# Two attention blocks side by side: VectorE's part of phi placed behind the next scores, the first q and k written in pieces, 25600 columns ahead of tile 0, and A's last q chains moved

## The chip, the cores and the metric

The kernel runs on one core of a Trainium2 chip. Its engines run side by side, each with its own queue of instructions, and wait for each other through semaphores: TensorE (PE in the profile, its weight loads PEld), VectorE (DVE), ScalarE (ACT), GpSimd (POOL) and SyncE (SP, which here issues most DMAs). The metric is the time of one execution on the device in microseconds, the median of the timed runs. The profiler's span runs from the first to the last instruction and is a little shorter than that time.

## The reference

Two independent attention blocks A and B work on inputs of 2048 tokens by 640 columns, with 32 heads of 20 channels. Their outputs stand side by side in a result of 2048 by 1280.

```python
# A: causal attention in a window of 256
qkv = (x @ wqkv).reshape(B, S, 3, H, Dh)
scores = einsum("bhqd,bhkd->bhqk", q, k) * (Dh ** -0.5)
mask = (i - j >= 0) & (i - j < 256)
o = softmax(where(mask, scores, -1e9)) @ v
out_A = o.reshape(B, S, D) @ wo

# B: linear attention over all tokens
phi = lambda t: where(t > 0, t + 1, exp(t)) + 1e-6
pq, pk = phi(q), phi(k)
kv = einsum("bhsd,bhse->bhde", pk, v);  z = einsum("bhsd->bhd", pk)
o = einsum("bhqd,bhde->bhqe", pq, kv) / (einsum("bhqd,bhd->bhq", pq, z)[..., None] + 1e-6)
out_B = o.reshape(B, S, D) @ wo
```

## The kernel before

**Stages of 512 tokens.** Both blocks are cut into NS = 4 stages of SB = 512 tokens (TPS = 4 blocks of 128). A product with a weight matrix is a *chain* (`chain`, L201): KT = 5 matmuls that add up in one bank of PSUM, up to 512 columns wide. The pool `dps` has three such banks. `bank()` hands out the next one, so the chain of bank n+3 cannot start before bank n has been read. `evac` copies a bank to SBUF, on VectorE (L192) or, near the end, in turn with ScalarE (L190).

**A's tiles.** `a_rows` makes q or k of a stage with channels on the partitions: five chains of 128 channels, evacuated into the tile `st`. `bounce` writes `st` to a scratch in DRAM (L267), and four DMAs read it back (L271) into `qpad` or `kpad`, where each head has its own rows. `a_v` makes v. The scores of a stage are cut into units, 90 in all (`tiles_of`): eight or sixteen small matmuls into the only tile `S_ps` (L574), one Exp of ScalarE over 128x2048 into `p` (L582), a mask by GpSimd (`affine_select`, L596), and two units later 16 matmuls `O_ps` of p with v (L618). Where a group of units ends, VectorE takes the reciprocal of the sums (L640) and multiplies (`otokA`, L641). After the last group of a stage `otokA` is transposed by DMA into `oT` (L652), and `a_out` multiplies with wo.

**B's work.** `b_kv(s)` makes k in token rows with phi, v, and adds the products of both to `kv_acc`. `b_q(s)` makes q with phi, channels on the partitions, and a DMA transpose `tok<-phi` (L498) of each of its five chains. `b_den`, `quotients` (L534 and the DMA transposes of L537), `b_merge` and `b_out` divide and project. `kv_ready` runs steps of GpSimd and DMA between the chains of b_q(0).

**phi.** `phi` issues the Exp of a bank on ScalarE (L210) at once. Its remaining part, two instructions of VectorE (L214, `e<-e`; L217, `phi<-dense,e`), is put into the list `later`. `flush` issues what is in that list. Before, `evac` called it behind its copy, and `phi` behind its own Exp; so the pair of a bank came right after the next evacuation or the next phi. The pair reads the bank, so the bank comes free only after it.

**The order of the work** is written out by hand. `fill` is one long generator over all chains. First come a_v(0) and q and k of A's stage 0. Then `take(EARLY)` runs EARLY columns of `fill` ahead of the first scores. From there on, each unit takes an equal share of what is left: `rate = (FILL - TAIL - ...) / 90` columns behind the O_ps matmuls of the unit two before it. `spread` mixes quarters of the transposing loads of the next x (L689) into a generator, one each `step` yields; `even` interleaves two generators bank by bank; `drip` does so with the reads of `bounce`. SP's queue is in order, so a DMA that waits holds all behind it.

**The start.** SP loads x of A's stage 0 in two halves and A's weights by thirds. TensorE first runs 40 dummy matmuls on the identity (`warm_up`, L150), which GpSimd makes; then it transposes x (L134) and starts a_v(0).

**The end.** `b_out(3)` and `a_out_last` (four output DMAs of SP, L673) run behind the last units.

Of the kernel before, what the change touches and what calls it, by code (L numbers as in the profile page):

```python
# [9 lines left out]
P = 128  # L10
# [6 lines left out]
H = 32  # L17
# [6 lines left out]
EARLY = 33280  # L24
FILL = 350080
# [29 lines left out]
def kernel(  # L55
# [52 lines left out]
    def load_w(n, src, i, eng):  # L108
        wv = src.rearrange("(kt p) n -> p kt n", p=P)
        eng.dma_start(  # L110
            out=w_sb[n][:, :, i * D : (i + 1) * D], in_=wv[:, :, i * D : (i + 1) * D]
        )
# [33 lines left out]
    def warm_up():  # L146

        ps = dps.tile([P, SB], F32, name="dense")
        for _ in range(40):
            nc.tensor.matmul(ps[:, 0:P], lhsT=ident[:], rhs=ident[:], start=True, stop=True)  # L150
# [24 lines left out]
    later = []  # L175

    def flush():

        while later:
            later.pop(0)()  # L180
# [3 lines left out]
    def evac(dst, src, to=None):  # L184
# [8 lines left out]
        flush()  # L193

    def bank():
        return dps.tile([P, SB], F32, name="dense")
# [10 lines left out]
    def phi(dst, src, view=lambda t: t[:], then=None):  # L207

        e = ep.tile([P, SB], BF16, name="e")
        nc.scalar.activation(out=view(e), in_=src, func=ACT.Exp)  # L210
        flush()
# [11 lines left out]
        later.append(rest)  # L223
# [38 lines left out]
    def bounce(n, s, st, dst):  # L262


        scratch = tc.dram_tile([D, SB], BF16, name=f"{n}_scr{s}")
        eng = nc.scalar if s == 0 else nc.sync
        eng.dma_start(out=scratch.rearrange("(c p) n -> p c n", p=P), in_=st[:])  # L267
# [21 lines left out]
    def a_rows(n, s):  # L289
        base = 0 if n == "q" else D  # L290
        st = stp.tile([P, KT, SB], BF16, name="st")
        for c in range(KT):
# [7 lines left out]
            evac(st[:, c, :], ps[:])  # L300
            if c == KT - 1:
                pad, pl, name = (q_pad, qp, "qpad") if n == "q" else (k_pad, kp, "kpad")
                pad[s] = pl.tile([P, NG, SB], BF16, name=name)
                bounce(n, s, st, pad[s])
# [15 lines left out]
    def v_proj(n, xt, dst):  # L320
        hh = H // 2
        for tb in range(TPS):
            for i in range(2):
                ps = bank()
                yield from chain(
                    ps[:, 0 : hh * DH],
                    lambda kt: xt[:, kt, tb * P : (tb + 1) * P],
                    lambda kt: w_sb[n][:, kt, 2 * D + i * hh * DH : 2 * D + (i + 1) * hh * DH],
                    hh * DH,
                )  # L330
                evac(
                    dst[:, tb, i * hh : (i + 1) * hh, 0:DH],
                    ps[:, 0 : hh * DH].rearrange("p (h d) -> p h d", d=DH),
                )
                yield End(hh * DH)
# [380 lines left out]
    for i in range(2):  # L716
        load_w("A", A_wqkv, i, nc.sync)
# [120 lines left out]
```

## Time and profile before

| | |
|---|---|
| median of three timed runs | 281.84 us (279.88, 281.84, 284.75) |
| the profiled execution | 280.25 us |
| its span | 278.5 us |
| PE busy | 266.9 us, 96% |
| ACT, DVE, POOL busy | 201.8, 172.7, 163.1 us |
| the Exp of a unit (L582) | 90 x 1875 ns |
| O_ps matmuls (L618) | 1440, 50.9 us |
| phi on VectorE (L214, L217) | 40 x 0.39 us and 40 x 0.69 us |
| first scores at | 38.12 us |

A line of the profile names the source line of the kernel, the engine, the operation and `written<-read` tiles; `x8` is a count, `[0.79 <-DMA xB]` an idle time ahead of the instruction and what ended it. A `q` behind an engine's name (SPq, ACTq) marks its sequencer, which issues DMAs. A window has, for each engine, its busy time and count. The timed runs of this kernel spread over 1.7%.

### The profile page before, as it was taken

The numbers are of one execution on the slowest core, as the hardware profiler recorded it, in microseconds if no ns is written. First come the engines' busy times: TensorE is split into PE (matmuls) and PEld (weight loads), VectorE is DVE, ScalarE is ACT, GpSimd is POOL, SyncE is SP. The second block draws the span as 40 slices with busy tenths as digits, with TensorE's granted clock in tenths as the row PEclk, the third lists the DMA queues.
The fourth block names the chain that finished last, engine by engine and source line by source line (L and its number), as shares of the span: only waits on it lengthen the run. The fifth ranks groups of instructions, "written<-read, shape, count | busy, mean of one in ns | idle before, by whom it ended". The sixth has DMA issues, their size and how long they took to land.

```text
span 278.5 us, 8218 instructions
## 1 busy us (share of the span) xinstructions
PE 266.9 (96%) x3474; PEld 155.3 (56%) x3516; DVE 172.7 (62%) x336; ACT 201.8 (72%) x231; POOL 163.1 (59%) x204
## 2 busy tenths in 40 slices
PE   7999999999999999999999899999999999999995
PEld 7744465665665654565664354465644564456542
DVE  0656665657757555554566576987688767866821
ACT  1200039989989887889989899778889889998432
POOL 5000017667656667776669956676687778777710
PEclk9999999999999999999999999999999999999999
DMA  7997596949532994541016624599979744940886
GB/s 248 305 308 215 157 233 164 175 89 201 158 74 47 138 126 113 142 120 34 2 26 120 106 50 101 133 163 192 173 121 151 111 134 126 116 117 28 167 193 209
DMA packets 81214, 38.88 MB, mean 140 GB/s; under 512 B 63897, under 2 KB 80281, under 8 KB 81177
## 3 DMA queue, kind: packets, MB, share of 16 engines
q1 hardware_dynamic: 78857, 32.45, 57.7%
q0 software_dynamic: 1008, 4.59, 5.0%
q10 hardware_dynamic: 1312, 1.31, 1.4%
q8 instruction: 27, 0.44, 0.7%
q14 instruction: 10, 0.08, 0.2%
HBM read 12.45 MB, written 10.49 MB: 82 GB/s over the span
## 4 chain that ended last, share of the span: by engine, by line
PE 82%; ACT 7%; DVE 3%; issue 3%; DMA 2%; POOL 1%; DVEq 0%; POOLq 0%; SPq 0%; ACTq 0%
PE dense L201 52%; PE O_ps L618 14%; PE S_ps L574 10%; ACT p L582 6%; PE dense L415 2%; PE dense L150 2%; DMA xA<-vB 1%; DMA xB<-in_B_x_dram 1%; POOL p L596 1%; PE dense L464 1%; DVE otokA L641 1%; ACT e L210 1%; PE dense L134 1%; DVE tok L534 1%; DVE st L192 0%
## 5 line engine op out<-in xcount | busy, mean ns | idle before, releaser
L596 POOL TENSOR_SCALAR_AFFINE_SELECT p<-p 128x512 bf16<-128x512 bf16 (+1 forms) x180 | 150.9, 839 | 100.7 <-ACT p L582 93.6
L582 ACT ACTIVATE p<-S_ps 128x2048 bf16<-128x2048 f32 x90 | 168.7, 1875 | 39.5 <-PE S_ps L574 39.0
L618 PEld LDWEIGHTS <-p 128*128 128x128 bf16 x1440 | 42.3, 96 | 20.2 <-issue 16.9
L618 PE MATMUL O_ps<-vA,p 128*128 128x21 bf16 x1440 | 50.9, 173 | 1.1 <-DVE otokA L641 0.6
L201 PE MATMUL dense<-wB,xB 128*128 128x320 bf16 (+2 forms) x310 | 48.1, 296 | 1.0 <-DVE vB L192 0.3
L201 PE MATMUL dense<-xA,wA 128*128 128x512 bf16 x191 | 45.3, 379 | 0.6
L192 DVE CAST st<-dense 128x512 bf16<-128x512 f32 x40 | 27.5, 690 | 22.5 <-PE dense L201 19.5
L574 PE MATMUL S_ps<-qpad,kpad 20*128 20x256 bf16 (+2 forms) x736 | 35.9, 269 | 0.9 <-ACT p L582 0.4
L192 DVE CAST osb<-dense 128x512 bf16<-128x512 f32 (+1 forms) x35 | 22.5, 642 | 20.7 <-PE dense L201 19.2
L201 PEld LDWEIGHTS <-xA 128*128 128x128 bf16 x320 | 26.5, 97 | 15.1 <-DMA xA<-vB 1.6
L201 PEld LDWEIGHTS <-xB 128*128 128x128 bf16 x320 | 26.0, 97 | 13.3 <-issue 1.3
L574 PEld LDWEIGHTS <-kpad 20*128 20x128 bf16 x736 | 12.7, 92 | 30.5 <-issue 29.0
L201 PEld LDWEIGHTS <-wA 128*128 128x128 bf16 x200 | 18.5, 97 | 19.9
L217 DVE SCALAR_TENSOR_TENSOR phi<-dense,e 128x512 bf16<-128x512 f32 x40 | 27.7, 692 | 1.4
L567 ACT ACTIVATE p<-ident 1x1 bf16<-1x1 bf16 x90 | 16.9, 188 | 15.4 <-DVE st L192 15.4
L201 PE MATMUL dense<-wB,xA 128*128 128x512 bf16 (+1 forms) x155 | 24.5, 296 | 1.0 <-DMA xA<-vB 0.6
L201 PE MATMUL dense<-xB,wB 128*128 128x512 bf16 x89 | 24.2, 378 | 1.3 <-DMA xB<-in_B_x_dram 0.8
L210 ACT ACTIVATE e<-dense 128x512 bf16<-128x512 f32 x40 | 23.6, 593 | 1.3 <-PE dense L201 0.9
L192 DVE CAST vB<-dense 128x320 bf16<-128x320 f32 x32 | 15.3, 489 | 14.7 <-PE dense L201 14.2
L201 PE MATMUL dense<-woA,oT 128*128 128x128 bf16 (+1 forms) x153 | 23.4, 295 | 0.8 <-DVE osb L192 0.5
L201 PE MATMUL dense<-wA,xA 128*128 128x320 bf16 x160 | 23.9, 299 | 0.1
L192 DVE CAST vA<-dense 128x320 bf16<-128x320 f32 x32 | 15.8, 492 | 9.4 <-PE dense L201 9.3
(41 smaller groups left out, 150.4 us busy)
## 6 DMA issues: line engine op xcount, KB each, us to landing
out_dram<-osb POOLq DMA_DIRECT2D x7, 640.0 KB, 4.3
qpad<-q_scr SPq DMA_DIRECT2D x16, 160.0 KB
kpad<-k_scr SPq DMA_DIRECT2D x16, 160.0 KB
wA<-in_A_wqkv_dram SPq DMA_DIRECT2D x3, 800.0 KB
wB<-in_B_wqkv_dram SPq DMA_DIRECT2D x3, 800.0 KB
q_scr<-st SPq DMA_DIRECT2D x3, 640.0 KB
k_scr<-st SPq DMA_DIRECT2D x3, 640.0 KB
woA<-in_A_wo_dram SPq DMA_DIRECT2D x1, 800.0 KB
```

The costliest lines, as they stand in the source:

```text
L134: nc.tensor.transpose(ps[:, c * P : (c + 1) * P], tok[:, tb, c * P : (c + 1) * P], ident[:])
L150: nc.tensor.matmul(ps[:, 0:P], lhsT=ident[:], rhs=ident[:], start=True, stop=True)
L192: nc.vector.tensor_copy(out=dst, in_=src)
L201: nc.tensor.matmul(dst, lhsT=lhs(kt), rhs=rhs(kt), start=(kt == 0), stop=(kt == KT - 1))
L210: nc.scalar.activation(out=view(e), in_=src, func=ACT.Exp)
L217: nc.vector.scalar_tensor_tensor(out=dst, in0=src, scalar=0.0, in1=view(e), op0=ALU.max, op1=ALU.add)
L415: nc.tensor.matmul(pv[:, i, :, :], lhsT=pk[:, tb, c * P : (c + 1) * P], rhs=vB[:, tb, GH * c : GH * c + NHC, :], start=(tb == 0), stop=(tb ...
L567: nc.scalar.activation(out=p_all[0:1, 4 * SB : 4 * SB + 1], in_=ident[0:1, 0:1], func=ACT.Copy)
L574: nc.tensor.matmul(S_ps[:, j, blk * P : blk * P + n], lhsT=kt[32 * j : 32 * j + DH, g, ko : ko + P], rhs=q_pad[s][32 * j : 32 * j + DH, g, ...
L582: nc.scalar.activation(out=p, in_=S_ps[:], func=ACT.Exp, scale=scale)
L596: nc.gpsimd.affine_select(out=v, in_=v, pattern=[[0, 4], [0, b1 - b0], [sgn, P]], compare_op=ALU.is_ge, fill=0.0, base=0 if kind == "D" el ...
L618: nc.tensor.matmul(O_ps[:, slot, j, :], lhsT=p[:, j, b * P : (b + 1) * P], rhs=v_tok[kb // TPS][:, kb % TPS, 4 * gg + j, :], start=(first ...
```

## The change

There are five parts.

1. **phi.** `evac` and `phi` no longer call `flush`. The tile loop calls it right behind each `scores`, ahead of `values`. Each entry of `later` carries the number of its bank, and `bank()` flushes the entries that are two banks old, so that a bank has been read when its turn comes again.
2. **First q and k.** In stage 0, each chunk of 128 channels is written to the scratch by its own DMA of ScalarE's queue, right behind its evacuation, five for q and five for k instead of one each. The reads wait for all five. Other stages are as before.
3. **The start.** The dummies read a zeroed tile (a memset of VectorE, in a buffer of `osb`) instead of the identity; 28 run ahead of the first transposes and 3 behind them. A's v weights come in two halves, the first ahead of the second half of x, and a_v(0) takes the first columns of token blocks 0 and 1 before the others.
4. **Columns.** EARLY falls from 33280 to 25600 columns, and FILL rises by the same 7680: the share of a unit goes from 3668 to 3753 columns.
5. **A's stage 3.** Its five q chains (`banks(early, KT)`) run ahead of b_kv(3), no longer between the chains of b_q(0). The five k chains alternate one by one with b_q(0), and the quarters of B's next x are issued at each of the first yields (step 1, before 4).

The last output of A uses a buffer of `otokA`, no longer of `osb`.

```diff
-EARLY = 33280
-FILL = 350080
+EARLY = 25600
+FILL = 357760
...
-    def warm_up():
-
+    def warm_up(wait):
+
+        z = op.tile([P, TPS, D], BF16, name="osb")
+        nc.vector.memset(z[:, 0, 0:P], 0.0)
         ps = dps.tile([P, SB], F32, name="dense")
-        for _ in range(40):
-            nc.tensor.matmul(ps[:, 0:P], lhsT=ident[:], rhs=ident[:], start=True, stop=True)
+        for n in wait:
+            for _ in range(n):
+                nc.tensor.matmul(
+                    ps[:, 0:P], lhsT=z[:, 0, 0:P], rhs=z[:, 0, 0:P], start=True, stop=True
+                )
+            yield
...
     later = []
-
-    def flush():
-
-        while later:
-            later.pop(0)()
+    begun = [0]
+
+    def flush(before=None):
+
+        while later and (before is None or later[0][0] <= before):
+            later.pop(0)[1]()
...
             nc.vector.tensor_copy(out=dst, in_=src)
-        flush()

     def bank():
+        flush(begun[0] - 2)
+        begun[0] += 1
         return dps.tile([P, SB], F32, name="dense")
...
         nc.scalar.activation(out=view(e), in_=src, func=ACT.Exp)
-        flush()
...
-        later.append(rest)
+        later.append((begun[0], rest))
...
-    def bounce(n, s, st, dst):
-
-
-        scratch = tc.dram_tile([D, SB], BF16, name=f"{n}_scr{s}")
-        eng = nc.scalar if s == 0 else nc.sync
-        eng.dma_start(out=scratch.rearrange("(c p) n -> p c n", p=P), in_=st[:])
+    def bounce(n, s, scratch, st, dst):
+
+
+        if s > 0:
+            nc.sync.dma_start(out=scratch.rearrange("(c p) n -> p c n", p=P), in_=st[:])
...
             evac(st[:, c, :], ps[:])
+            if s == 0:
+                nc.scalar.dma_start(out=scratch[c * P : (c + 1) * P, :], in_=st[:, c, :])
...
+        order = by_tokens
+        if s == 0:
+            order = [(0, 0), (1, 0), (0, 1), (1, 1), (2, 0), (2, 1), (3, 0), (3, 1)]
+        yield from v_proj("A", xA[s], v_tok[s], order)
...
     load_half(0)
-    load_w("A", A_wqkv, 2, nc.sync)
+    load_w("A", A_wqkv, 2, nc.sync, 0, hh * DH)
     load_half(1)
+    load_w("A", A_wqkv, 2, nc.sync, hh * DH, D)
...
-    warm_up()
+    dummies = warm_up((28, 3))
+    next(dummies)
     transposes(0)
+    next(dummies)
...
         k_reads(2, a_v(2)),
+        banks(early, KT),
         b_kv(3),
-        spread(even(q[0], KT, early, 3), [("B", NS + 1)], 4),
+        spread(even(q[0], KT, early, KT), [("B", NS + 1)], 1),
...
         p = scores(okey[0], parts)
+        flush()
```

45 lines of the change are left out of this document (22 added, 23 removed).

## The prediction

> **What bounds the kernel now.** First the busy table, the slices and the chain of the page.
>
> ```profile
> PE 266.9 (96%) x3474; PEld 155.3 (56%) x3516; DVE 172.7 (62%) x336; ACT 201.8 (72%) x231; POOL 163.1 (59%) x204
> ...
> PE   7999999999999999999999899999999999999995
> ...
> PEclk9999999999999999999999999999999999999999
> ...
> PE 82%; ACT 7%; DVE 3%; issue 3%; DMA 2%; POOL 1%; DVEq 0%; POOLq 0%; SPq 0%; ACTq 0%
> ```
>
> TensorE is full in every slice but the first and the last two, and 82% of the chain is its own work. So an edit gains only where TensorE stands still or does work that is no part of the result. The waits of PE name the standing:
>
> ```profile
> PE dense L150 <- POOL ident masks.py:199: 1.4, 1, 1.4
> PE dense L201 <- DMA xB<-in_B_x_dram: 0.8, 1, 0.8
> PE O_ps L618 <- DVE otokA L641: 0.6, 1, 0.6
> PE dense L201 <- DMA xA<-vB: 0.6, 1, 0.6
> PE dense L201 <- DVE osb L192: 0.5, 1, 0.5
> PE O_ps L618 <- POOL p L596: 0.4, 1, 0.4
> ```
>
> They are few and short. Measured from start to start of the matmul records, against the usual 0.216 us of a 512-column matmul, the places that lose over 0.25 us are 93.6 us (0.47), 153.9 (0.57), 157.4 (0.95), 177.1 (0.71), 220.4 (0.65), 255.0 (0.26) and 266.4 (0.72): 4.3 us together. With the head this is all that can be won.
>
> **The head.** Windows over the first microseconds (busy time and count of PE, PEld, DVE, ACT, POOL):
>
> ```profile
> 1.43:5.67 4.24, 4.24 (x41) 4.24 (x42) 0.00 (x0) 0.66 (x1) 2.78 (x5) 1.00 0.88 292
> 5.67:6.99 1.32, 1.27 (x12) 1.00 (x11) 0.49 (x1) 0.01 (x1) 0.00 (x0) 1.00 1.06 377
> 6.99:13.18 6.19, 6.19 (x50) 4.52 (x51) 3.83 (x8) 1.39 (x2) 0.00 (x0) 1.00 1.15 328
> ```
>
> The 40 dummy matmuls take 4.24 us, 0.106 each. After 6.99 us the same 128 columns take 0.056: TensorE runs at half speed until there, and although the column of the granted clock says 1.00, the record of that clock begins only at 6.99. By the packets in the trace the first half of x has landed at 3.47, long before the first transpose at 5.67.
>
> Changed: the dummies no longer wait for the identity (ready at 1.37) but for a memset of VectorE. The other engines' first instructions start at 0.81; the memset is bounded by POOL's first fills (0.10) and VectorE's memset of 220 words (0.24), and the hand-over takes 0.05, so 1.05 is taken. 28 x 0.106 brings the first transpose to 4.02 (was 5.67), still behind the landing by 0.55. Ten transposes (1.06) and three dummies (0.32) end at 5.40; xA's first copy, 0.78 + 0.49 behind the first transpose as before, is ready at 5.34. The first chain starts at 5.40, not 6.99: 1.59 earlier, but at half speed until the clock opens at a time T. The gain is then (T - 5.40)/2 - (T - 6.99) = 4.29 - T/2: 0.80 if T stays at 6.99, 0.99 if it keeps its distance from the first matmul (6.61), 1.59 at the most, nothing from T = 8.6. Weights: wA's v part, 800 KB, landed 2.23 us behind x; its first half lands at 4.6 if bytes count, at 5.7 if packets count (0.15 lost); I take bytes, since 1280-byte packets pass at 287 and 1024-byte ones at 342 per us. I take **-0.9**, with -1.6 and +0.9 (an opening 3.4 us later than 6.99) as ends.
>
> The Trainium skill (TensorE: Matmul & The Clock Gate, Part 1) says that the gate opens after one busy window of about 3.4 us whose phase is free-running. By it T lies 3.4 to 6.8 us behind the first matmul, 4.5 to 7.9, and the term between -1.6 and -0.3; the 5.56 us seen here agrees.
>
> **7680 columns moved behind the first tile.** The dense stretch before tile 0 ran 33280 columns in 13.8 us; 7680 fewer are 3.2 us, which return as 7680/90 = 85 columns (0.036 us) in each unit. PE's total is the same, so 0, if the first scores find their operands. These lines show that:
>
> ```profile
> 24.90 0.37 ACTq L267 DMA_DIRECT2D k_scr<-st  x1
> ...
> 31.16 1.48 SPq L271 DMA_DIRECT2D kpad<-k_scr  x4
> ...
> 38.12 0.40 PE L574 MATMUL S_ps<-qpad,kpad 20*128 20x128 bf16 x16
> ```
>
> The k write took 5.84 us to land (30.74), beside the q reads (24.4 to 29.3), and the last k read landed at 36.45, 1.67 before use. Now scores are due at 38.12 - 0.9 - 3.2 = 34.0. The last k channels leave VectorE at 23.96; only 128 packets are then to be written. Alone, q's write took 1.66 us to its first packet and 1.87 for 640 packets; a fifth of that, doubled for the q reads beside it, is 0.75: landed near 26.8 with the issue. Reads issue at 27.1 and need 5.3 as before: 32.4, 1.6 before use. The eight more issues on ACT are 8 x 0.39 = 3.1 us, in an idle time of 15.4 and 13.1 us there. By the order of semaphores k's second write waits for xB's first load (21.33), about 1.6 us with only the later writes behind it. SP's q reads follow from about 21, not 23.46. Term **0**; ends 0 and +4.0 (below).
>
> A shorter dense share also left ScalarE as the bound in some units: p takes 1.88 and the next S_ps starts 0.05 behind its end in about half of the 89. But PE's last step before it is only 0.02 longer there than in the others, some 1 us in all; no gain is counted.
>
> **phi's VectorE part.** 40 pairs, 0.28 to 0.80 + 0.69, keep their number; only their place in VectorE's order moves. An evacuation stands right before the pair in 36 cases, in 28 after the change; a reciprocal of the tile loop stands right behind the pair in 14, and in 13 after. What is queued behind a pair is that reciprocal (0.26) and otokA's product (0.49), for which the next O_ps waits; at 151.8 to 153.9 that sequence left 0.67 us. The pair can wait for nothing but its Exp, which keeps its place behind the chain on ScalarE. The nearest rows of a loss and a gain are 177.1 (+0.71) and 93.6 (-0.47). I take **0**: the counts hardly move.
>
> ```profile
> L214 DVE TENSOR_SCALAR e<-e x40: 282/332/801, 43.4 to 246.3; 128x512 bf16<-128x512 bf16 x40
> ```
>
> The rows at 0.80 lie over POOL's selects for 0.73 us, those at 0.28 for at most 0.22. The Trainium skill (SBUF — State Buffer, Who interferes with whom) has a rule for it, against this change: such a VectorE form and GpSimd hold one port pair exclusively, so the later one waits. The trace agrees, 0.80 against 0.28. Its price is a rival below.
>
> **A's last q chains earlier, B's load closer.** The largest loss of the tile phase:
>
> ```profile
> 153.67 1.64 SPq L498 DMA_TRANSPOSE tok<-phi  x1
> ...
> 155.35 1.28 SPq L689 DMA_TRANSPOSE xB<-in_B_x_dram  x1
> ...
> 158.56 1.46 PE L201 MATMUL dense<-xB,wB 128*128 128x512 bf16 x6 [0.79 <-DMA xB<-in_B_x_dram]
> ```
>
> q[1] of B waits for the fourth quarter of its x, which SP issued behind oT's four transposes (5.2 us) and a tok transpose that waited for phi. In the new order the four quarters stand together behind oT, before any tok transpose, and ten chains (25600 columns, 6.8 units, 17 us) lie between b_kv(3) and q[1] instead of eight. Four issues of 1.28 and 3.1 us to land are 8.2: hidden. **-0.95**. What is late next is the 177.1 loss, whose tok products stay. With the chains move a q_scr write (issue 0.59, now ahead of oT, whose output projection is tens of us later), four qpad reads between tok transposes, and k's write and reads, whose wait (6 us at 188) holds tok transposes as before. kpad's last part landed at 200.2 for the unit of 202.4; its reads now stand about 23,000 columns earlier. No PE wait is added there.
>
> The tail's order of instructions is unchanged; the last A output takes another buffer, whose reader is long done: 0.
>
> **Sum.** -0.9 - 0.95 = -1.85. The profiled execution took 280.25 (278.5 of span, 1.75 around): 278.4. The timed runs were 279.88, 281.84 and 284.75; the profiled one lies 1.6 under their median. Taken off the middle of all four (281.05), the forecast is 279.2.
>
> **Rivals**, from the same 281.05:
> - *The head gives nothing* (T at 8.6 or later; x landing late eats the 0.55 us left): 281.05 - 0.95 = 280.1. For it: how the clock opens is seen once only.
> - *The x wait only moves*: SP, behind k's write or oT, delays another transpose by as much: 280.15. For it: SP's own waits for k_scr sum to 19.1 us. Against: the 8 us to spare.
> - *More goes*: the other losses (2.7 without 157.4 and the tail's 0.7 at 266.4, which hangs on unchanged transposes) were phases of one pattern and vanish: 276.5. Against: every new order has its own.
> - *Slower, at the first scores*: five small writes land one behind the other, 5 x 1.66 = 8.3 us instead of 5.84. k's reads then land at 36.45 - 0.9 + 2.5 = 38.0, TensorE stands 4.0 us from 34.0: 283.2. It is slower than before from a stand of 1.85 us. For it: the longest wait in the slack that is spent; against: q's write alone, 1.87 us of packets.
> - *Slower, at the reciprocals*: each of 13 is pushed by 0.52 (0.80 - 0.28) through POOL and no slack is left: +6.8, 286.0. It decides from 0.14 each. Against: the 0.67 us of slack.
>
> **How the numbers follow.** Forecast 0.48; head nothing 0.12; x wait moves 0.12; more 0.12; first scores 0.10; reciprocals 0.06. The range 276.5 to 282.6 takes in the first four and the milder half of the slow ones. A measurement tells about 2% (5.6 us): under 276.2 needs more than the larger gain, 0.06; over 287.5 needs the last rival and a slow median, 0.04; within 0.90.
>
> **What would show it.** Right: first transpose near 4.0; first S_ps near 34 with no idle time before it from kpad; no wait for xB; the same tail. Wrong: an idle PE before the first S_ps, T late, or several waits on otokA.

## The result, and the profile after

The changed kernel takes **289.45 us** (median of four, 287.74 to 291.96) against 280.89 us of the kernel before on the same chip: a ratio of **1.029** with a 95% interval of 1.021 to 1.036. The forecast was 279.2 with a range up to 282.6; to more than 287.5 it gave a chance of 0.04. The profiled execution took 288.95 us, with a span of 287.3. Ratios, here and below, are taken from undisturbed executions only, so that they need not be the quotient of the medians.

First the page's busy line, the slices of PE and of its clock, and the shares of the chain that ended last, of the changed kernel.

```profile
PE 271.8 (95%) x3507; PEld 154.9 (54%) x3507; DVE 172.1 (60%) x337; ACT 202.1 (70%) x231; POOL 163.8 (57%) x204
...
PE   8999669999999999999999999998899999999993
...
PEclk9999989999999999999999999999999999999999
...
PE 70%; DMA 11%; ACT 5%; DVE 4%; SPq 3%; issue 3%; POOL 3%; ACTq 0%; DVEq 0%; POOLq 0%
```

The share of DMA in the chain was 2% and is 11%. Slices 5 and 6 of PE (28.7 to 43.1 us) were full and are at six tenths, and the clock's sixth slice is at eight. So a loss stands where the first scores begin, behind a transfer. The list of waits of PE names it:

```profile
PE S_ps L587 <- DMA kpad<-k_scr: 2.7, 3, 1.0
PE dense L208 <- DVE st L198: 2.5, 2, 2.2
PE dense L208 <- DMA oT<-otokA: 1.6, 2, 1.3
PE dense L152 <- DVE osb L148: 1.1, 1, 1.1
PE dense L477 <- DVE wB L198: 0.9, 1, 0.9
PE dense L208 <- DVE osb L198: 0.9, 4, 0.3
PE dense L208 <- DMA wA<-in_A_wqkv_dram: 0.5, 1, 0.5
```

The forecast's second loss, the wait for xB, is gone as foretold. Of the new lines the first two, 5.2 us together, lie ahead of the first Exp. The timeline (start, length, what, and in brackets the idle time ahead and its releaser) shows the path from the start to the first scores:

```profile
19.44 0.33 ACTq L309 DMA_DIRECT2D q_scr<-st  x1
...
20.52 8.92 ACTq L309 DMA_DIRECT2D k_scr<-st  x5
...
26.84 1.52 SPq L277 DMA_DIRECT2D qpad<-q_scr  x4
...
34.53 1.48 SPq L277 DMA_DIRECT2D kpad<-k_scr  x4
34.67 2.71 DVE L198 CAST st<-dense 128x512 bf16<-128x512 f32 x4 [4.00 <-DMA k_scr<-st]
35.41 2.32 PE L208 MATMUL dense<-xA,wA 128*128 128x512 bf16 x10 [2.24 <-DVE st L198]
...
39.04 0.23 PE L587 MATMUL S_ps<-qpad,kpad 20*128 20x128 bf16 x1 [1.01 <-DMA kpad<-k_scr]
40.13 0.23 PE L587 MATMUL S_ps<-qpad,kpad 20*128 20x128 bf16 x1 [0.86 <-DMA kpad<-k_scr]
41.23 0.60 PE L587 MATMUL S_ps<-qpad,kpad 20*128 20x128 bf16 x13 [0.88 <-DMA kpad<-k_scr]
```

ScalarE's queue takes 8.92 us over five k writes that were counted at 0.39 each. By the packets the last k write lands at 34.04 (before: 30.74, though it was issued as late as 24.90). Two things wait for that landing. k's reads are issued at 34.53, for scores that were due at 34.0. And stage 1's `st` takes the buffer that the k write still reads, so VectorE's evacuation waits 4.00 us, the three banks fill, and PE stands for 2.24 us in chains that have nothing to do with the scores.

The windows over the head, the stand for `st` and the half clock (length, then busy time and count of PE, PEld, DVE, ACT, POOL; then clock, DMA share and GB/s):

```profile
1.06:4.03 2.97, 2.97 (x28) 2.90 (x29) 0.00 (x0) 1.03 (x1) 2.94 (x6) 1.00 0.66 192
4.03:5.67 1.64, 1.58 (x16) 1.42 (x14) 0.49 (x1) 0.34 (x1) 0.18 (x1) 1.00 1.06 303
5.67:6.73 1.06, 1.06 (x5) 0.59 (x5) 0.00 (x0) 0.36 (x1) 0.00 (x0) 1.00 0.81 250
6.73:13.12 6.39, 5.78 (x47) 3.98 (x46) 3.93 (x8) 0.70 (x1) 0.00 (x0) 1.00 1.12 299
33.18:35.41 2.23, 0.00 (x0) 0.00 (x0) 0.74 (x2) 0.00 (x0) 0.00 (x0) 1.00 0.07 22
40.86:44.27 3.41, 3.04 (x23) 1.81 (x24) 0.49 (x1) 1.96 (x2) 0.45 (x1) 0.50 1.03 259
```

The first transposes start at 4.03, as worked out (4.02), but the q chains start at 13.12, where they started at 13.18. The fourth line has TensorE busy for 5.78 of 6.39 us; the line of before that ends with the q chains had 6.19 of 6.19. And the last line is new: from 40.86 to 44.27 us TensorE has half its clock, from within the third stand for kpad on. The mean granted clock of the four executions was 0.993, 0.982, 0.994 and 0.982. One such spell takes 0.006 off it (half of 3.41 us in 287.3), so two of the four had about three.

The whole, by stretches of the span. Units are counted from 0; a stretch runs from the Exp of one unit to that of another. The forecast moves -0.9 and -3.2 into the first row, spreads the 3.2 over the 90 units, and takes 0.95 from the third.

| stretch | before | forecast | after | after less forecast |
|---|---|---|---|---|
| start to the first Exp | 38.58 | 34.48 | 41.87 | +7.4 |
| units 0 to 45 | 110.64 | 112.24 | 112.03 | -0.2 |
| units 45 to 63 | 45.86 | 45.55 | 46.88 | +1.3 |
| units 63 to 89 | 63.47 | 64.39 | 64.88 | +0.5 |
| unit 89 to the end | 19.95 | 19.99 | 21.64 | +1.7 |
| span | 278.5 | 276.65 | 287.3 | +10.7 |

Two thirds of the miss stand ahead of the first Exp.

### The profile page after: what moved, and what is told of

Its sections match the earlier page's. It is cut to its first block, busy times and chain, and to the rows that moved or that the text cites. A ratio compares the mean times of both kernels' runs of the same rounds, so it can differ in the third digit from the quotient of the medians.

```text
span 287.3 us, 8277 instructions
## 1 busy us (share of the span) xinstructions
PE 271.8 (95%) x3507; PEld 154.9 (54%) x3507; DVE 172.1 (60%) x337; ACT 202.1 (70%) x231; POOL 163.8 (57%) x204
## 4 chain that ended last, share of the span: by engine, by line
PE 70%; DMA 11%; ACT 5%; DVE 4%; SPq 3%; issue 3%; POOL 3%; ACTq 0%; DVEq 0%; POOLq 0%
PE dense L208 45%; PE O_ps L631 13%; PE S_ps L587 9%; ACT p L595 4%; DMA oT<-otokA 3%; DMA q_scr<-st 3%; DMA wA<-in_A_wqkv_dram 2%; SPq L665 2%; DMA kpad<-k_scr 2%; DMA k_scr<-st 2%; PE dense L428 2%; POOL p L609 2%; DVE osb L198 1%; POOL wB L169 1%; DVE st L198 1%
## 5 line engine op out<-in xcount | busy, mean ns | idle before, releaser
L208 PE MATMUL dense<-xA,wA 128*128 128x512 bf16 x200 | 46.9, 379 | 2.5 <-DVE st L198 2.5
L208 PE MATMUL dense<-wB,xB 128*128 128x320 bf16 (+2 forms) x320 | 48.5, 299 | 0.0
L198 DVE CAST st<-dense 128x512 bf16<-128x512 f32 x40 | 27.2, 689 | 25.0 <-PE dense L208 18.4
L587 PE MATMUL S_ps<-qpad,kpad 20*128 20x256 bf16 (+2 forms) x736 | 36.7, 271 | 3.5 <-DMA kpad<-k_scr 2.7
L208 PEld LDWEIGHTS <-xA 128*128 128x128 bf16 x320 | 27.2, 99 | 17.3 <-DMA xA<-vB 1.2
L208 PEld LDWEIGHTS <-xB 128*128 128x128 bf16 x320 | 26.0, 97 | 11.9
L198 DVE CAST osb<-dense 128x512 bf16<-128x512 f32 x31 | 21.3, 687 | 16.6 <-PE dense L208 16.4
L208 PEld LDWEIGHTS <-wA 128*128 128x128 bf16 x200 | 18.5, 97 | 22.9 <-issue 3.1
L224 DVE SCALAR_TENSOR_TENSOR phi<-dense,e 128x512 bf16<-128x512 f32 x40 | 27.7, 692 | 1.4
L208 PE MATMUL dense<-woA,oT 128*128 128x512 bf16 (+1 forms) x160 | 25.0, 299 | 2.7 <-DMA oT<-otokA 1.6
L208 PE MATMUL dense<-wA,xA 128*128 128x320 bf16 x160 | 26.1, 313 | 0.7 <-DMA wA<-in_A_wqkv_dram 0.5
L208 PE MATMUL dense<-xB,wB 128*128 128x512 bf16 x100 | 26.6, 378 | 0.0
L208 PE MATMUL dense<-wB,xA 128*128 128x512 bf16 (+1 forms) x160 | 25.3, 299 | 0.2 <-DMA xA<-vB 0.2
L198 DVE CAST vA<-dense 128x320 bf16<-128x320 f32 x32 | 15.7, 490 | 16.4 <-PE dense L208 16.3
L221 DVE TENSOR_SCALAR e<-e 128x512 bf16<-128x512 bf16 x40 | 16.3, 408 | 14.6 <-ACT e L218 14.2
```

The costliest lines, as they stand in the source:

```text
L198: nc.vector.tensor_copy(out=dst, in_=src)
L208: nc.tensor.matmul(dst, lhsT=lhs(kt), rhs=rhs(kt), start=(kt == 0), stop=(kt == KT - 1))
L221: nc.vector.tensor_scalar(out=e[:], in0=e[:], scalar1=1e-6, scalar2=1.0 + 1e-6, op0=ALU.add, op1=ALU.min)
L224: nc.vector.scalar_tensor_tensor(out=dst, in0=src, scalar=0.0, in1=view(e), op0=ALU.max, op1=ALU.add)
L587: nc.tensor.matmul(S_ps[:, j, blk * P : blk * P + n], lhsT=kt[32 * j : 32 * j + DH, g, ko : ko + P], rhs=q_pad[s][32 * j : 32 * j + DH, g, ...
```

## The experiments

The theory after this reading: the dense work ahead of tile 0 was the cover of k's way through DRAM; the change takes 3.2 us of it away and at the same time lengthens that way. The rivals: phi's new place or A's moved chains cost something, the split writes alone cost it, the new head alone. So the parts were tried alone and in steps. Ratios are to the kernel before on the same chip, with 95% intervals; the kernel before had medians of 280.58 to 282.00 on these chips.

### phi's place alone

The kernel before, with part 1 of the change and nothing else.

```diff
             nc.vector.tensor_copy(out=dst, in_=src)
-        flush()
...
     def bank():
+        flush(begun[0] - 2)
+        begun[0] += 1
...
         p = scores(okey[0], parts)
+        flush()
```

> The kernel before with phi's pair behind the next scores, nothing else. The kernel with this and A's moved chains took 278.64 us against 280.71. Theory (the gain comes from the moved chains, which take the 0.95 us wait for x and the other losses between 150 and 180 us away; phi's place moves nothing): 280.2 to 281.2. Rival (phi's place frees the banks sooner and gains by itself): 279.5 or less.

279.25 us, ratio **0.994** (0.990 to 0.997): phi's place gains about 1.8 us by itself, where the forecast had put 0. Its waits of PE:

```profile
PE dense L203 <- DMA xA<-vB: 0.8, 1, 0.8
PE O_ps L619 <- POOL p L597: 0.8, 2, 0.4
PE dense L203 <- DMA xB<-in_B_x_dram: 0.8, 1, 0.8
```

The kernel before had 0.5 behind `DVE osb` and 0.3 behind `DVE vB` (a bank that waited for its evacuation); they are gone, with the stands at 93.6 and 220.4 us. The wait for xB is still there. By stretches it gains 1.03 us in units 0 to 45, 0.25 to 63 and 0.53 to 89. (The 0.71 ahead of the first Exp is not counted: the clock opened at 4.74 in this execution and at 6.99 in that of the kernel before.)

How the gain comes about shows at 93.6. First four lines of the kernel before, then one of the kernel with phi and A's chains:

```profile
92.95 0.26 DVE L640 RECIPROCAL recA<-O_ps 128x16 f32<-128x16 f32 x1 [1.76 <-PE O_ps L618]
...
93.65 0.48 DVE L192 CAST vB<-dense 128x320 bf16<-128x320 f32 x1
...
94.05 0.28 DVE L214 TENSOR_SCALAR e<-e 128x512 bf16<-128x512 bf16 x1
94.19 0.84 PE L201 MATMUL dense<-wB,xB 128*128 128x320 bf16 x5 [0.31 <-DVE vB L192]
```

```profile
92.24 0.37 DVE L215 TENSOR_SCALAR e<-e 128x512 bf16<-128x512 bf16 x1 [1.29 <-ACT e L212]
```

Before, the Exp of the pair had ended at 92.45 and VectorE was idle until 92.95, but the pair was only issued behind the next evacuation, and its bank stayed taken until 95.06. With the new place the pair runs in that idle time, and its bank is free at 93.40.

### phi and A's chains

With part 5 added (the five q chains ahead of b_kv(3), quarters of x from step 1).

```diff
         k_reads(2, a_v(2)),
+        banks(early, KT),
         b_kv(3),
-        spread(even(q[0], KT, early, 3), [("B", NS + 1)], 4),
+        spread(even(q[0], KT, early, KT), [("B", NS + 1)], 1),
```

> The kernel before with two parts of the change alone: phi's pair behind the next scores, and A's last q chains ahead of B's last key stage with B's x quarters at the first yields. Theory (these two parts gain the 0.95 us of the x wait and cost nothing else): 279 to 280.5 against 280.9 before, no wait for xB near 157. Rival (the loss is here, through longer waits for VectorE's evacuations as seen near 198 us in the changed kernel): 283 to 289.

278.64 us (278.20 to 279.67), ratio **0.993** (0.991 to 0.995). No wait for xB is left. New is 0.9 us behind `DVE wB`, which the changed kernel has too, so what A's chains add to phi's 1.8 us is small: 0.6 between the medians, not separable by the intervals. It has the lowest median here, 2 us below the kernel before on its chip, and is called the fastest kernel below. The loss is not in these two parts.

### One write each for q and k

The next runs undo or shift one thing in the changed kernel. First the five small writes become one again, as before the change; all else stays.

```diff
-            if s == 0:
-                nc.scalar.dma_start(out=scratch[c * P : (c + 1) * P, :], in_=st[:, c, :])
...
-        if s > 0:
-            nc.sync.dma_start(out=scratch...
+        eng = nc.scalar if s == 0 else nc.sync
+        eng.dma_start(out=scratch...
```

> The changed kernel with q and k of stage 0 written by one DMA each again, as before the change; all else of the change stays. Theory (the loss of 8.6 us sits before tile 0: the small writes of ScalarE's queue share the DMA engines with B's first x transposes, and k's second write waits for the semaphore of that load): the x transposes run at their old rate again and k's write lands near 32 instead of 34.04; the first scores (due near 35) still wait some 2 to 4 us for k, 283 to 286 us. Rival (five small writes are slow in themselves): k is back to the 5.8 us of before, with the same 283 to 286. Rival (the loss is phi's new place or A's moved chains): no change, 288 to 290.

285.48 us, ratio 1.019 (1.015 to 1.023): 3 to 4 us less than with five. k's write has landed at 27.9, six microseconds earlier than the five (some 32 had been expected), and its reads are issued at 28.58. PE still stands 1.9 us at the first scores, and the wait for `st` is gone. So the split writes are the worse way for k, and without them there is still a loss.

### Which of the waits holds the small writes

In the changed kernel every DMA of SP and of ScalarE's queue takes one of eight semaphores in turn, and waits until the DMA that had it last has landed. The second write of k shares its semaphore with the first load of B's x. This run adds one write of 256 bytes behind the first write of q. It shifts the turn by one, so that k's second write shares with another DMA; the added work is one issue. The turn of every later DMA is shifted with it.

```diff
                 nc.scalar.dma_start(out=scratch[c * P : (c + 1) * P, :], in_=st[:, c, :])
+                if n == "q" and c == 0:
+                    tiny = tc.dram_tile([1, P], BF16, name="tiny")
+                    nc.scalar.dma_start(out=tiny[:, :], in_=st[0:1, 0, 0:P])
```

> The changed kernel with one more write of 256 bytes to a scratch of its own behind the first write of q, which shifts the rota of eight DMA semaphores by one: k's second write now waits for q's first write and no longer for the load of B's x; everything else stays. Theory (this wait holds k's writes): k's writes issue one per k chain, end by 30 instead of 34.04, and the stand before the first scores shrinks by 3 to 4 us: 283.5 to 286. Rival (the DMA engines are simply full until 27 us, the semaphore adds nothing): k's writes still end after 32.5, 288 to 290.

285.30 us, ratio 1.015 (1.006 to 1.024). With one more DMA the median is 4 us lower. Between the two profiled executions (span 283.3 against 287.3) 2.6 us of the gain lie ahead of the first Exp, which comes at 39.29 and not 41.87, and 1.5 behind unit 89, where no run settles the cause. The timeline:

```profile
22.30 2.64 ACTq L309 DMA_DIRECT2D k_scr<-st  x5
...
27.39 1.52 SPq L277 DMA_DIRECT2D qpad<-q_scr  x4
30.68 1.48 SPq L277 DMA_DIRECT2D kpad<-k_scr  x4
```

The five k writes take 2.64 us of the queue and not 8.92, and the last one lands at 27.7 and not 34.04. PE no longer waits for `st`. So the wait that holds the small writes is that for xB's first load, which ends at 26.87. (Freed of it, they also land ahead of q's reads, beside which they lay before.) k's reads now wait for the first read of q (landed at 30.7), which has the semaphore of k's first read. PE stands 3.2 us for kpad, and the half clock comes at 38.61.

### wv in one load, and xB's load later

Two more that undo one thing each. First A's v weights in one load again.

```diff
-    load_w("A", A_wqkv, 2, nc.sync, 0, hh * DH)
+    load_w("A", A_wqkv, 2, nc.sync)
     load_half(1)
-    load_w("A", A_wqkv, 2, nc.sync, hh * DH, D)
```

> The changed kernel with A's v weights loaded in one piece again; all else stays. The 640-byte pieces took 0.034 us each against 0.062 for 1280 bytes in the packets, but every load behind them landed 1 to 3 us later. Theory: loads land 1.5 us earlier (A's second x by 13.5, B's weights by 20), the k write lands 1.5 to 3 us earlier, the first scores stall by 2 to 3 us less: 285 to 287 us. Rival (the halves cost nothing, only contention of the small writes counts): 288.5 to 289.5.

286.61 us, ratio 1.023 (1.019 to 1.026). B's first x now lands at 24.9 and k's last write at 31.6 (26.9 and 34.0 in the changed kernel). Set beside the other runs this splits the lateness of that load: 21.3 before, 25.1 with the halves and one write each, 24.9 with the small writes and wv whole, 26.9 with both. The halves push it by 3.8 us, the small writes by 3.6, both together by 5.6. A half moves pieces of 640 bytes where the whole moves 1280; in the trace of the changed kernel such a packet takes 32 ns in the median, one of 1280 bytes 55 ns.

Then B's first x loaded behind the reads of k.

```diff
-    run(load("B", 0))
...
-    for n in "qk":
-        drop((n, 0))
+    drop(("q", 0))
+    drop(("k", 0))
+    run(load("B", 0))
```

> The changed kernel with the load of B's first x issued behind the reads of k instead of ahead of q's writes; all else stays. Theory (order of issue: k's writes 2 to 5 wait for that load's semaphore, and both share the engines): k's writes end by 27.5, its reads by 33, no stand at the first scores, no closed clock near 41: 280 to 282 us. Rival (small writes are slow in themselves): k's writes still end after 31 and the first scores stand over 2 us: 285 or more.

283.60 us, ratio 1.012 (1.007 to 1.017), slower than expected. With B's x out of the way the fourth of the five k writes lands at 25.2, but the last one takes until 28.9, beside the reads of q. k's reads leave at 29.64, and PE stands for 1.77 us. The half clock comes at 37.16.

### 33280 columns in the changed kernel

```diff
-EARLY = 25600
-FILL = 357760
+EARLY = 33280
+FILL = 350080
```

> The changed kernel with 33280 columns ahead of tile 0, as before the change. Its reads of k landed at 41.2 us in the changed kernel, its first scores would now be due at about 41. Theory (the first scores come too early for k): the stand of 2.7 us there and the half clock behind it (3.4 us, 1.7 lost) go, the 2.2 us wait for a free stage tile stays: 284 to 286. Rival (where the scores start does not matter, PE loses as much elsewhere): 288 to 290.

282.76 us, ratio 1.007 (1.002 to 1.011): 6 us of the changed kernel's loss go with this one number, more than was expected. There is no stand at the first scores and, in the profiled execution, no half clock (three of the ten executions have a mean clock of 0.994). It is the cover that matters. PE stands 1.95 us for `st` at 33.5 and 2.2 us in the head, so the new head and the split writes still cost.

### The other parts, one at a time on the fastest kernel

Each is added to the kernel with phi and A's chains (0.993). First the dummies on a zeroed tile, 28 and 3.

```diff
-            nc.tensor.matmul(ps[:, 0:P], lhsT=ident[:], rhs=ident[:], start=True, stop=True)
+                    ps[:, 0:P], lhsT=z[:, 0, 0:P], rhs=z[:, 0, 0:P], start=True, stop=True
...
-    warm_up()
+    dummies = warm_up((28, 3))
+    next(dummies)
     transposes(0)
+    next(dummies)
```

> The kernel with phi's and A's parts (278.64 us) and the new dummies alone (28 and 3, on a zeroed tile); A's v weights are loaded in one piece, 33280 columns ahead of tile 0. Theory: the first chain waits for the whole of the v weights, landed at 5.7, so it starts at 5.75 at half speed, some 0.6 us gained at most and less where the clock opens late: 277.8 to 279. Rival (the shorter warm-up leaves the clock closed for longer and loses): 279.5 to 281.

279.30 us, ratio 0.995 (0.992 to 0.997). In the profiled execution the first chain waits 2.57 us for A's v weights, until 7.47, not 5.75 as expected, and the clock is halved from 7.40 to 10.81; ten of the other eleven executions have a mean clock of 0.998 or more. To it wv in halves and a_v(0)'s new order were added.

```diff
-    load_w("A", A_wqkv, 2, nc.sync)
+    load_w("A", A_wqkv, 2, nc.sync, 0, hh * DH)
     load_half(1)
+    load_w("A", A_wqkv, 2, nc.sync, hh * DH, D)
...
+            order = [(0, 0), (1, 0), (0, 1), (1, 1), (2, 0), (2, 1), (3, 0), (3, 1)]
```

> As the run with the new dummies, with A's v weights in two halves around the second half of x and the first chains in the other order. Theory (the second half of x and of the weights land at 7.8 and 9.0 us, and TensorE stands 1 to 2 us at 7 to 9): 0.5 to 1.5 us slower than with whole weights, and the later loads, 1.5 to 2 us late, still reach tile 0 at 33280 columns in time: 278.5 to 280.5. Rival (the halves gain what was forecast): 277 to 278.

278.86 us, ratio 0.996 (0.992 to 0.999). The new head gives nothing that can be measured, in either form. Next the split writes alone, with the old head.

```diff
+            if s == 0:
+                nc.scalar.dma_start(out=scratch[c * P : (c + 1) * P, :], in_=st[:, c, :])
```

> The kernel with phi's and A's parts (278.64 us) and q and k of stage 0 written by five DMAs each, 33280 columns ahead of tile 0, the start as before. Theory (the writes share the engines with the load of B's x, and k's second write waits for that load's semaphore): the load ends near 24 instead of 21.3, k's writes near 32 instead of 30.9, the stage tile of A's next k comes free later and TensorE stands 0.5 to 1.5 us near 32; the first scores just hold: 279 to 281. Rival (small writes bring q and k sooner): k's writes end by 28, time as without them or up to 0.5 us less.

279.54 us, ratio 0.998 (0.995 to 1.000): a cost of about 1.3 us by the ratios, with intervals that meet. k's writes end at 31.7 and PE stands 1.15 us for `st`. With 33280 columns and the old head that is all they cost. Last, 25600 columns alone, with one write each and the old head.

```diff
-EARLY = 33280
-FILL = 350080
+EARLY = 25600
+FILL = 357760
```

> The kernel with phi's and A's parts (278.64 us) and, in addition, 25600 columns ahead of tile 0 instead of 33280; q and k of stage 0 are written by one DMA each, the start is that of before. k's reads landed near 36.5, its scores are due at 34.9. Theory: TensorE stands 1.5 to 2 us there, and if the clock closes loses up to 1.7 more: 280 to 282.5. Rival (the smaller share before tile 0 gains elsewhere as much, because ScalarE is then never the bound): 278 to 279.

284.47 us, ratio **1.011** (1.007 to 1.015), 5 us over 0.993 and more than expected. Its timeline at the first scores:

```profile
31.15 1.48 SPq L272 DMA_DIRECT2D kpad<-k_scr  x4
...
34.25 0.22 PE L575 MATMUL S_ps<-qpad,kpad 20*128 20x128 bf16 x1
35.37 0.22 PE L575 MATMUL S_ps<-qpad,kpad 20*128 20x128 bf16 x1 [0.89 <-DMA kpad<-k_scr]
36.52 0.23 PE L575 MATMUL S_ps<-qpad,kpad 20*128 20x128 bf16 x1 [0.93 <-DMA kpad<-k_scr]
37.55 0.39 PE L575 MATMUL S_ps<-qpad,kpad 20*128 20x128 bf16 x13 [0.80 <-DMA kpad<-k_scr]
```

k's path is that of before (its reads left at 31.16 there); the scores come earlier, at 34.25, and wait 2.6 us for the second, third and fourth read. Then the clock halves from 38.57 to 41.98, some 1.7 us of work. By stretches, against the fastest kernel and with the moved columns taken off, the loss is 2.6 us ahead of the first Exp, 1.4 in units 0 to 45 (the half clock), none to 63, 1.0 to 89 and 0.4 behind: 5.4 between the two profiled executions.

So one at a time, on the fastest kernel, the columns cost 0.018 of the ratio, the small writes 0.0045 and the new head 0.003, together 0.025. The changed kernel lies 0.036 above it. The remaining 0.010, some 3 us, comes only with the parts together. It is a rough figure, as the interval of the changed kernel's ratio alone is 0.008 either way. A likely reason, not tested apart, is the load of B's x, which the halves and the small writes both push back and for which a k write waits.

### How the number of columns acts behind the first scores

The same kernel with 30720 columns was thought to pay little more than the stand.

```diff
-EARLY = 33280
-FILL = 350080
+EARLY = 30720
+FILL = 352640
```

> The kernel with phi's and A's parts (278.64 us), q and k written by one DMA each, and 30720 columns ahead of tile 0: scores are due near 37.1, k's reads land near 36.5. Theory (the loss of fewer columns is the stand before the first scores and the half clock behind it): neither shows, 278 to 279.5. Rival (a third of it comes later, from how the columns fall between the units near 190 to 208 us): 279.5 to 281, with the five waits of 0.2 us for evacuations there.

283.66 us, ratio 1.009 (1.005 to 1.013). The stand is 0.80 us and the profiled execution has no half clock, and yet it took 282.83 us, 4.2 more than that with 33280 (278.63). (Six of the twelve executions have a mean clock of 0.993 or 0.994 and took 284.4 to 285.5 us, the other six 281.8 to 282.9; with 33280 no execution is under 0.998.) The waits of PE show where the 4.2 are:

```profile
PE O_ps L619 <- DVE otokA L642: 2.1, 2, 1.1
...
PE dense L203 <- DVE phi L218: 1.0, 2, 0.5
PE dense L465 <- DVE rden L523: 1.0, 1, 1.0
PE dense L203 <- DMA xA<-vB: 0.9, 1, 0.9
PE S_ps L575 <- DMA kpad<-k_scr: 0.8, 1, 0.8
```

Units 45 to 63 took 49.45 us against 46.00 with 33280 columns, and the columns that were moved there account for only 0.2 of it (18 units of 28 columns). Three more runs ask whether this is a matter of which unit B's merge chains meet. Two give the missing columns back in the first 45 units, so that behind unit 45 every chain stands where it stands with 33280; the third shifts the other way (35840). The first:

```diff
-EARLY = 33280
+EARLY = 30720
+BACK = 2560
...
+        if i < 45:
+            credit += BACK / 45
         credit -= take(credit)
```

> The kernel with phi's new place and A's moved q chains, with 30720 columns ahead of tile 0, but the 2560 columns are handed out on top of the old share in the first 45 units (57 each), so that from unit 45 on every chain stands where it stands with 33280. If the 3.3 us that 30720 lost in units 50 to 63 are a matter of how B's merge chains fall against the units, they are gone: about 0.8 us of stand at the first scores is left, 279.3 to 280. If the loss belongs to the first scores or to the later loads, the time stays at 283 to 284.

279.69 us, ratio **0.996** (0.992 to 1.000). Units 45 to 63 take 46.00 again and 63 to 89 take 62.94. Its waits are those of the fastest kernel with the stand for kpad added:

```profile
PE dense L204 <- DMA xA<-vB: 1.3, 2, 0.9
PE dense L466 <- DVE wB L194: 0.9, 1, 0.9
PE S_ps L576 <- DMA kpad<-k_scr: 0.9, 1, 0.9
PE O_ps L620 <- DVE otokA L643: 0.7, 1, 0.7
```

The same for 25600 (BACK = 7680):

> The same with 25600 columns ahead of tile 0 and 7680 handed out over the first 45 units (171 each). The stand at the first scores (2.6 us) and the half-clock spell (1.7) stay, the loss behind unit 50 goes: 282.5 to 283.3. If the units with the larger share become late themselves (ScalarE's Exp and the share no longer fit in 2.4 us), 284 or more.

283.03 us, ratio 1.005 (1.001 to 1.009), against 1.011 without the return. Units 63 to 89 fall from 64.88 to 62.94, where the columns explain 0.92 of the 1.94. The stand (2.0) and the half clock (38.21 to 41.62) stay.

And 35840, with nothing given back:

```diff
-EARLY = 33280
-FILL = 350080
+EARLY = 35840
+FILL = 347520
```

> The same kernel with 2560 columns more ahead of tile 0, 35840, at the small share. If the columns ahead of tile 0 only have to cover the transfer of k, more of them bring nothing: 278.6 plus or minus 0.5 at unchanged alignment. If the number moves the merge chains against the units, it can come out 1 to 3 us longer, with the loss in units 50 to 63 and none at the first scores.

285.45 us, ratio **1.019** (1.013 to 1.024): more columns ahead of tile 0 are as bad as fewer, and worse than expected. The first Exp comes at 39.59, without a stand. The loss is spread: 1.3 us in units 0 to 45, 2.5 to 63, 1.3 to 89, 1.7 behind them, each over what 0.993's kernel would take less the moved columns. The clock halved from 193.87 to 197.28, behind stands of 0.37, 0.90 and 0.85 us.

The stretches of the kernels that show it best, in us (columns: first Exp, units 0 to 45, 45 to 63, 63 to 89, behind, span of the profiled execution):

| kernel | first | 0-45 | 45-63 | 63-89 | behind | span |
|---|---|---|---|---|---|---|
| phi's place | 37.87 | 109.61 | 45.61 | 62.94 | 19.77 | 275.8 |
| phi and A's chains | 38.59 | 109.33 | 46.00 | 62.95 | 20.03 | 276.9 |
| the same, 25600 | 37.98 | 112.39 | 46.61 | 64.88 | 20.44 | 282.3 |
| 25600, given back | 37.21 | 113.45 | 46.10 | 62.94 | 21.70 | 281.4 |
| the same, 30720 | 38.37 | 110.04 | 49.45 | 63.43 | 19.81 | 281.1 |
| 30720, given back | 38.05 | 110.42 | 46.00 | 62.94 | 20.49 | 277.9 |
| the same, 35840 | 39.59 | 110.09 | 48.32 | 63.91 | 21.69 | 283.6 |
| changed, one write each | 37.69 | 110.87 | 46.62 | 64.88 | 23.64 | 283.7 |
| changed | 41.87 | 112.03 | 46.88 | 64.88 | 21.64 | 287.3 |

Two rows hold a half clock in their last stretch: the changed kernel with one write each (272.22 to 275.63), and, not in the table, the one with the halves (268.62 to 272.03). The first column also moves with the opening of the clock: the first two kernels run the same program up to their first Exp, the clock opens at 4.74 and 6.56 us, and the Exp comes at 37.87 and 38.59.

A stretch of the tile phase repeats to 0.02 us wherever the chains stand alike, whatever was done to the head: units 63 to 89 take 62.93 to 62.95 in seven of the kernels. In every kernel with 25600 columns not given back they take 64.87 or 64.88; three of the four chains of A's output projection that wait for an evacuation lie there (`PE dense L208 <- DVE osb L198: 0.9, 4, 0.3` in the changed kernel, 0.74 us of it behind unit 63).

## Why the prediction was wrong

**What bounds it** was right: TensorE, and losses only where it stands. The chains are the same, and the span is 8.8 us longer. Idle time of PE grew by 3.9 us (11.6 to 15.5) and its busy time by 4.9; half clock and the records of lone matmuls count as busy, and the 4.9 were not apportioned further.

**7680 columns: 0.** This step failed, and it is most of the miss. It needed k's reads landed by 32.4 with scores due at 34.0; the last one landed at 41.2. Three sizes in it were wrong:
- *The wait for xB's load.* It was seen (about 1.6 us) but sized with xB's landing in the kernel before, 21.33. In the changed kernel xB lands at 26.87, since the halves and the small writes push it back. Without that wait (one more DMA) the last write landed at 27.7, not 34.04, and the first Exp came at 39.29, not 41.87.
- *The small write*, 0.75. The last of the five took 4.8 us where it lay beside q's reads (issued near 24.1, landed at 28.9, with xB's load out of the way). An issued write's row alone (1.66 to its first packet) did not bound it.
- *The reads*, 5.3 us. The prediction took the last landing from the packets, 36.45, with 1.67 us to spare. The semaphore that the scores wait for was raised at 37.66 in the trace of the kernel before: 6.5 us behind the first issue, with 0.46 to spare. In the changed kernel the reads are issued at 34.53, that semaphore is raised at 41.18, and the last scores start at 41.23.

The forecast had +4.0 as the upper end of this term. The first Exp came 7.4 later than forecast. The head's missing 0.84 and the stands for `st` (2.24 and 0.31) put the due time of the scores at 37.4. The last of them start at 41.23: 3.8 us for k's reads, of which 2.74 are recorded as idle; the rest is the wait of the first weight load and the records of three lone matmuls (0.23 each). The half clock adds about 0.2: the Exp follows the start of the last 13 by 0.64, where it followed that of all 16 by 0.46 before. The evacuation that waits for `st` was not in the sum at all: the kernel before has that wait too (1.0 us on VectorE at k's write), but there the banks covered it.

**The split in five was to bring k earlier, and brought it later.** The rival "slower, at the first scores" had the place, with a chance of 0.10, but less than half the size (283.2, 4.0 above the forecast, where 10.25 were measured). Its mechanism, writes that land one behind the other, is part of what happened (the first five landings of that queue lie between 21.2 and 26.3, 1.3 us apart in the mean); the larger part is the shared semaphore: without it the last k write landed 6.3 us earlier. Even with one write each, 25600 columns cost 5 us, so that rival would have come without the split.

**The head: -0.9.** The first transposes were right to 0.01 us, with some luck: the semaphore of x's first half was raised at 3.99, 0.04 ahead of them, where 0.55 had been counted on. The count by bytes was nearly right: the first half of wv landed at 4.83 (4.6 by bytes, 5.7 by packets). The first chain came at 5.67, not 5.40. The three dummies start 0.107 apart, as counted, but the chain follows the last one by 0.37; why was not settled. The clock opened at 6.73. By the formula of that step this still leaves (6.73 - 5.67)/2 + 0.26 = 0.79. What failed is that the sum stopped at the first chain: TensorE then waited 0.16 for the second half of x and 0.45 for the second half of wv, which landed at 8.65 where the whole wv had landed at 5.70. The q chains start 0.06 earlier; the remaining 0.1 was not assigned. Nor was it priced that the halves delay every load behind them.

The Trainium skill (TensorE: Matmul & The Clock Gate, Part 1) puts the opening after one busy window of about 3.4 us of free-running phase. By the traces the phase is free and the window is 3.41 us, but a window need not be wholly busy: the opening came between 2.64 us (25600, given back) and 5.67 us (changed) behind the first matmul, so the estimate of 3.4 to 6.8 that stood in the prediction was too late at its near end.

**phi's place: 0.** Wrong by -1.8 us, on the better side. The counts of instructions were right, but the step priced only what stands behind the pair (the reciprocals). It did not price the bank that the pair holds. The row of a gain was named (93.6, -0.47) and not taken: there the pair stood behind the next evacuation while VectorE was idle, and PE waited for a bank. This stand and that of 220.4 (0.65) make 1.1 of the 1.8; the rest was not assigned. The rival of the reciprocals (286.0) fell with it: the run of phi alone shows no such loss.

**The wait for xB: -0.95.** The mechanism was right: the wait is gone in every kernel with part 5. What is late next came at another place than the one named: 0.9 us behind `DVE wB` in the merge. So the net was small, nearer to the rival "the x wait only moves".

**No gain and no loss behind the first scores.** Wrong: the moved columns set which unit each later chain meets. In the changed kernel this is the 1.0 us in units 63 to 89 beyond the columns' own 0.92 (the run that gives them back takes it away). The 1.7 us of the tail, 1.3 of it one wait for oT's transpose (282.39), were not settled: the same program behind unit 89 took 20.03 us in the profiled execution of one kernel and 23.29 in that of the kernel with the halves, whose medians are 0.2 apart. A half clock (268.62 to 272.03) is part of the latter; the changed kernel has none there.

## What to carry to other kernels

Work ahead of a consumer is the cover of the transfer that feeds it; before that work is moved, take the transfer's whole path (the write, its place in the queues, the reads) against the new due time in the *changed* order, where its rivals in the DMA queues move too. A transfer cut into pieces is earlier only if no piece waits for another queue: count the semaphores it passes and what each shared one was last used for. In a schedule that is written out by hand, a single number (here 33280 columns) fixes how thousands of later instructions meet; shift it, and keep the later phase in place by giving the work back, or else the test measures two things at once.

## What the hardware showed unexpectedly

**The clock closes on a grid of 3.41 us, and three stands of a microsecond can be enough.** Half-clock spells that end before the work does last 3.41 us in each of the ten traces that have one, and begin at a whole number of windows of 3.413 us from the opening: 34.13 (ten) behind it in five kernels (the changed one: 6.73 to 40.86), and 3.41 (one), 30.72 (nine), 187.73 (55), 262.83 (77) and 266.24 (78) in one each. Seven of these spells (the five, and those after nine and after 55 windows) follow a window in which no single stand was longer than 1.01 us; its recorded idle time was 1.61 us (25600, given back) to 2.74 (one more DMA). Idle time alone does not give the limit, though: windows with 2.00 us of it (wv in one load, part of a stand of 2.44 us that ends at 274.05), 1.63 (25600, given back, 266.90 to 270.31) and 1.45 (one write each, at the first scores) did not close the clock. What decides between them stays open. The Trainium skill (TensorE: Matmul & The Clock Gate, Why this matters for your kernels) warns of gaps over about 3 us; the traces show that three gaps of a third of that are enough.

A spell costs about 1.7 us of work, half its length. Spells also come and go between executions of one kernel. Of the twelve with 30720 columns the six whose mean clock tells of one took 2.3 us longer in the mean (284.83 against 282.49); whether the 0.6 beyond the 1.7 are the stands that bring it on was not settled.

**A longer queue can be faster.** One more DMA of 256 bytes lowered the median by 4 us. It changed which load a later write had to wait for, and 2.6 us of the gain lie behind that write, ahead of the first Exp.

**Two halves of a load are dearer than the whole.** A 640-byte packet takes 32 ns in the median, a 1280-byte one 55 ns, so a byte takes 16% longer, and the second half, queued behind another load, landed 2.95 us later than the whole had.
